# Mask building, load sizes and task order in an mLSTM and two-MoE kernel

## The chip, the core and the metric

The kernel runs on one core of a Trainium2 chip. The metric is the device time of one execution in microseconds, lower is better. The core has TensorE (matmuls, called PE in the profile, with its weight loads as PEld), VectorE (DVE), ScalarE (ACT), GpSimd (POOL) and SyncE (SP), which issues most of the DMAs. Each engine works through its own list of instructions in order.

## The reference

Three stages in a row. The first is a recurrence over 768 time steps, for 2 batches and 8 heads of dimension 40; the other two are gated feed-forward layers over 1536 tokens of width 320 with a hidden width of 1536.

```python
for t in range(S):
    m_new = np.maximum(f_gate[:, :, t] + m, i_gate[:, :, t])
    f_stab = np.exp(f_gate[:, :, t] + m - m_new); i_stab = np.exp(i_gate[:, :, t] - m_new)
    C = f_stab * C + i_stab * outer(v_t, k_t);    n = f_stab * n + i_stab * k_t
    y[:, :, t] = sigmoid(o_gate[:, :, t]) * (C @ q_t) / np.maximum(np.abs(n @ q_t), 1.0)
x = (sigmoid(x @ w_gate) * (x @ w_val)) @ w_out      # first layer
x = ((x @ w_a) * (x @ w_b)) @ w_out                  # second layer
```

The feed-forward weights are 8-byte floating-point numbers, handed to the kernel as 64-bit integers.

## The kernel before

The recurrence is worked in 12 steps of 64 time steps (T = 64), over all 16 pairs of batch and head at once. For step s the kernel loads keys and queries (`load_kq`, tile kq) and values and keys by token (`load_kv`, tile Y), and makes a matrix of decay exponents on TensorE (`ph_E`, line 404): a product of lhsE and rhsE, in which the gate values V of the step stand in blocks, one per head, so that a mask is part of the data. ScalarE takes the exponentials (`ph_exp`, line 412, tile Dt), TensorE the key-query products (`ph_S`), VectorE multiplies both (`ph_P`, line 460). With keys weighted by decay (`ph_kw`, line 415) TensorE updates the state (`ph_st`, copied on ScalarE by `ph_state`, line 491) and makes the outputs (`ph_o`, line 479). These are normalised and gated (`ph_norm`, `ph_norm2`, line 507), transposed (line 517) and stored as a high and a low part in xb.

The decay blocks are filled in two ways. For steps 0 and 1 `ph_prep` multiplies V by a mask on VectorE (lines 378 and 384). For the later steps `ph_place` copies V into the blocks by ten small DMAs for each pair of steps, eight for rhsE (line 397) and two for lhsE (line 400), on SP's queue. The tables lhsE and rhsE are first copied from constants (cs) by ScalarE (lines 726 and 732); before, the second pair is zeroed by GpSimd.

Key-query products have two forms: for steps below NQ the queries are added to the same result by two identity matmuls (line 435), and the product with Dt covers both; from NQ on the queries are multiplied by Dt separately (`ph_qg`, line 425).

Each of the 24 weight tiles (128 rows of hidden width, 12 for each layer) is loaded by three DMAs (`load_w`, lines 248 to 250, tile wst), turned from 8-byte numbers into 4-byte ones (`narrow1` on ScalarE, lines 258 and 259; `narrow2a` to `narrow2c` on VectorE or GpSimd, lines 265 to 282), and split into a high part (`split1`, ScalarE) and low parts (`split2`, `split3`, lines 298 to 303). A unit of the feed-forward layers is one weight tile against two or four blocks of 128 tokens: two chains of matmuls (line 554: pa and pb), gate and product on ScalarE and VectorE, and a third chain (lines 561 to 563: acc). The first 24 units (HEAD) have two token blocks and run among the recurrence's steps.

The order on every engine is not written by hand. All work is a list of tasks, each with engines it may run on, a duration in nanoseconds, predecessors, buffers and a due time computed from a few constants. `order_tasks` runs this list through a model at build time: it takes, of the tasks that are ready, the one with the earliest start plus a small weight on its due time, and chooses among the allowed engines. Ready DMAs form a queue of their own ("D") whose model has an issue time and a wire time. The order so found is the program; at run time each engine waits only for true dependences. Where the model leaves TensorE idle ahead of the first feed-forward unit, `fill` issues dummy matmuls (line 208).

Of the kernel before, what the change touches and what calls it, by code (L numbers as in the profile page):

```python
# [50 lines left out]
SDUE0, SDUE = 17.7, 5.582  # L51
UDUE0, UDUE = 45.1, 3.871
CDUE = (15.5, 14.5, -5.422, 36.2)
CLEAD = -3.653
GDUE = (-1.384, -0.546, 39.8)
PLEAD = 10.2
SWITCH = 100
NQ = 6
MMDUE = 11.5
FGAP = 80  # L60
NFILL = 1
VBIAS = 563.4
SOFT, SOFTMAX = 0.017, 2291.8

HOLD = {4: "O7", 5: "O8", 6: "O9", 7: "O10", 8: "O11", 9: "O11"}
EDUE = 32.6
# [3 lines left out]
OGDUE = (-59.6, 21.1)  # L70
IDUE = 28.1
# [16 lines left out]

def tile_shape(name):

    return {"S": "T" if name[1] == "T" else "S", "O": "T", "Q": "S"}.get(name[0])


def order_tasks(tasks, bufs):
# [3 lines left out]
    port = wire = 0.0  # L98
    shape = None
# [8 lines left out]
    while ready:  # L108
        best = None
        for name in ready:  # L110
            on, _, after, due, uses, lock = tasks[name]
            new, held = {}, []
# [8 lines left out]
            for e, dur in on.items():  # L121
                t = max([free[e]] + [end[a] + hop(engine[a], e) for a in (*after, *held)])
# [40 lines left out]
def kernel(  # L163
# [75 lines left out]
    def load_w(c):  # L239
        l, f = divmod(c, NF)  # L240
        w, wo = ((w1, wo1), (w2, wo2))[l]
        k = 2 if wide else 1
        t = stpool.tile([P, NW * k], I32 if wide else F32, tag="wst", name=f"wst{c}")
        wo = wo[f * P : (f + 1) * P, :]
        w = w[f]
        if wide:
            w, wo = w.bitcast(I32), wo.bitcast(I32)
# [3 lines left out]
        wst[c] = t  # L251
# [122 lines left out]
    def ph_prep(s, eng):  # L374

        c0 = s * T
        re, ld = rhsE[0][:, s], lhsE[0][:, s]
# [30 lines left out]
    def ph_exp(s, par):  # L408

        if par == 0:  # L410
            Dt[s] = a2.tile([P, 2, NPAIR, B, T], F32, tag="Dt", name=f"Dt{s}")
        nc.scalar.activation(Dt[s][:, par], Eps[s, par].rearrange("p (a b t) -> p a b t", a=NPAIR, b=B), AF.Exp)

    def ph_kw(s, par, eng):
# [3 lines left out]
            Dt[s][:, par, :, :, T - 1 : T].to_broadcast([P, NPAIR, B, D]),  # L418
# [269 lines left out]
    BUFS = {"acc": 2, "mm1": 2, "e": 2, "y": 2, "dt": 2, "kq": 3, "xt": 2, "xb": 3, "g": 2, "gh": 2, "gl": 2,  # L688
# [21 lines left out]
    def t_start():  # L710
        load_gates(0)
        nc.scalar.dma_start(cs[:, C_RE:], cst[:, C_RE:])
# [6 lines left out]
    def dma(name, size, fn, after=(), due=0.0, uses=(), parts=1):  # L719

        task(name, "D", 480.0 * parts, fn, after, due, uses, lock=size / 0.29)

    dma("start", 300.0, t_start, (), -100, parts=2)
    dma("ident", 66.0, t_ident, ("start",), -88)
    def t_lhs(i):
        nc.scalar.activation(lhsE[i], cs[:, C_LD : C_LD + 2 * P].unsqueeze(1).to_broadcast([P, 2, 2 * P]), AF.Copy)
        if i:
            nc.gpsimd.memset(lhsE[i][32:64, :, T : T + P].bitcast(F32), 0.0)

    def t_rhs(i):  # L730
        r = slice(32 * i, P)
        nc.scalar.activation(rhsE[i], cs[:, C_RE : C_RE + 512].unsqueeze(1).to_broadcast([P, 2, 512]), AF.Copy)
        if i:
            nc.gpsimd.memset(rhsE[i][0:32].bitcast(F32), 0.0)
# [11 lines left out]
    for i, (c0, n) in enumerate(GCH):  # L746
# [8 lines left out]
        task(f"ge{i}", "A", 420 + 2.1 * n, c2, [f"gd{i}"], due + 0.3)  # L755
        task(f"gc{i}", "V", 220 + 1.05 * n, c3, [f"ge{i}"], due + 0.4, lock=True)
    for i in range(1, NSTEP // 2):
# [3 lines left out]
        dma(f"pl{i}", 130.0, lambda i=i: ph_place(i), src + ["rhs1", "lhs1"] + old, sdue(s) - PLEAD, parts=10)  # L761

    for s in range(NSTEP):
# [4 lines left out]
        dma("kq" + n, 328.0, lambda s=s: load_kq(s), ["start"], d - 12, [("kq", [z + n for z in ("S", *zs)])], parts=2)  # L768
# [22 lines left out]
        task("M" + n, "V", 500, lambda s=s: ph_norm2(s), ["N" + n], d + 5.2, lock=True)  # L791
# [184 lines left out]
```

## Time and profile before

| | us |
|---|---|
| median of 3 runs | 491.75 |
| lowest, highest | 491.3, 492.38 |
| the profiled execution | 492.37 |
| its span | 490.6 |
| TensorE busy in the span | 470.3 |
| VectorE, ScalarE, GpSimd busy | 286.2, 248.3, 126.0 |

The span is the time from the first to the last instruction in the profile, and a part of the execution's own time. Busy times are summed over the whole span; dummy matmuls count as TensorE's busy time. The profile also has the clock that TensorE was granted (1.00 is 2.4 GHz, 0.50 is 1.2 GHz) and the DMA engines' share of work in each stretch.

### The profile page before, as it was taken

What the parts mean: (1) busy time and instruction counts of PE and PEld (TensorE: products, weight loads), DVE (VectorE), ACT (ScalarE), POOL (GpSimd) and SP (SyncE); (2) the same over time, 40 slices, a digit from 0 to 9 for tenths busy, and PEclk for the clock granted to TensorE, in tenths of its full rate; (3) what the DMA queues carried; (4) which work ended last, traced back from release to release, by engine and by line L of the source; (5) the groups of instructions that cost most, each with busy time, mean ns of one, the idle gap of its engine ahead of it and who ended that gap; (6) DMA issues with size and microseconds to landing.
All of it is one profiled execution on the core that took longest, in us unless ns stands there. A gap on an engine that the chain in (4) does not pass through costs nothing.

```text
span 490.6 us, 9058 instructions
## 1 busy us (share of the span) xinstructions
PE 470.3 (96%) x3545; PEld 408.7 (83%) x3550; DVE 286.2 (58%) x474; ACT 248.3 (51%) x460; POOL 126.0 (26%) x141
## 2 busy tenths in 40 slices
PE   9969499999999999999999999999999999999995
PEld 3546498899999888888888888888888888888885
DVE  4785598957676768656555566754466323324242
ACT  5964595774788655555562543553454222222220
POOL 2314366554233103344240322231202000000000
PEclk9999799999999999999999999999999999999999
DMA  8944543920203332222311022220220000001022
GB/s 202 261 130 110 148 133 103 221 81 2 82 1 95 122 107 81 82 80 82 131 53 59 2 87 76 80 82 0 82 80 2 0 2 0 1 0 44 11 55 53
DMA packets 18506, 37.06 MB, mean 76 GB/s; under 512 B 3040, under 2 KB 9696, under 8 KB 18464
## 3 DMA queue, kind: packets, MB, share of 16 engines
q1 hardware_dynamic: 18048, 35.74, 25.0%
q10 hardware_dynamic: 416, 0.74, 0.7%
q8 instruction: 28, 0.46, 0.4%
q14 instruction: 14, 0.11, 0.1%
HBM read 34.35 MB, written 1.97 MB: 74 GB/s over the span
## 4 chain that ended last, share of the span: by engine, by line
PE 82%; DMA 9%; SPq 2%; DVE 2%; POOL 2%; issue 1%; ACT 1%; POOLq 0%; ACTq 0%; DVEq 0%
PE pa L554 29%; PE pb L554 22%; PE acc L561 9%; PE acc L563 8%; PE acc L562 8%; DMA x2tok<-in_ogate_dram 4%; DMA wst<-in_wo_dram 3%; SPq L397 1%; DMA Y<-in_kv_dram 1%; PE o L479 1%; PE sp L450 1%; PE t L517 1%; PE first L208 1%; DMA cs<-in_cst_dram 1%; POOL Kw L415 1%
## 5 line engine op out<-in xcount | busy, mean ns | idle before, releaser
L554 PE MATMUL pa<-xb,W 128*128 128x512 f32 (+1 forms) x864 | 172.3, 345 | 0.0
L554 PEld LDWEIGHTS pa<-xb,W 128*128 128x128 f32 x864 | 137.3, 190 | 15.9
L554 PE MATMUL pb<-xb,W 128*128 128x512 f32 x480 | 119.6, 392 | 0.0
L590 ACT ACTIVATE gh<-g 128x512 fp32r<-128x512 f32 (+1 forms) x84 | 47.9, 570 | 129.8 <-PE acc L562 107.8
L554 PEld LDWEIGHTS pb<-xb,W 128*128 128x128 f32 x480 | 89.9, 188 | 19.3
L584 DVE TENSOR_TENSOR g<-g,pb 128x512 f32<-128x512 f32 x60 | 41.3, 688 | 88.0 <-PE pb L554 86.2
L561 PE MATMUL acc<-W,gh 128*128 128x320 f32 x288 | 89.8, 312 | 0.0
L563 PE MATMUL acc<-W,gl 128*128 128x320 f32 x288 | 89.0, 309 | 0.0
L562 PE MATMUL acc<-W,gh 128*128 128x320 f32 x288 | 88.9, 309 | 0.0
L595 DVE TENSOR_TENSOR gl<-g,gh 128x512 fp32r<-128x512 f32 x60 | 44.4, 740 | 55.2 <-ACT gh L590 55.2
L579 ACT ACTIVATE g<-pa 128x512 f32<-128x512 f32 x60 | 35.8, 597 | 55.3 <-PE pa L554 55.1
L561 PEld LDWEIGHTS acc<-W,gh 128*128 128x128 f32 x288 | 54.0, 187 | 2.7
L562 PEld LDWEIGHTS acc<-W,gh 128*128 128x128 f32 x288 | 54.0, 188 | 2.4
L563 PEld LDWEIGHTS acc<-W,gl 128*128 128x128 f32 x288 | 54.0, 188 | 0.1
L282 POOL TENSOR_TENSOR wst<-cva,wst 128x960 int32<-128x960 int32 x11 | 25.2, 2290 | 66.6 <-DVE cva L276 32.7
L302 POOL TENSOR_TENSOR W<-wst,W 64x128 fp32r<-64x128 f32 x24 | 17.1, 711 | 91.7 <-ACT W L293 76.8
L258 ACT ACTIVATE cva<-wst 128x960 f32<-128x960 f32 x24 | 25.8, 1075 | 12.0 <-DMA wst<-in_wo_dram 11.8
L276 DVE SCALAR_TENSOR_TENSOR cva<-wst,cva 128x960 int32<-128x960 int32 x24 | 29.8, 1240 | 0.4
L595 POOL TENSOR_TENSOR gl<-g,gh 128x256 fp32r<-128x256 f32 x24 | 20.3, 844 | 36.3 <-ACT gh L590 26.4
L208 PE MATMUL first<-zb 128*128 128x512 bf16 x94 | 24.6, 416 | 1.5 <-DVE zb L212 1.2
L292 ACT ACTIVATE W<-wst 128x832 fp32r<-128x832 f32 x24 | 22.9, 955 | 6.1 <-DVE wst L282 5.1
L259 ACT ACTIVATE wst<-wst 128x960 int32<-128x960 uint32 x24 | 25.9, 1080 | 0.0
(83 smaller groups left out, 481.5 us busy)
## 6 DMA issues: line engine op xcount, KB each, us to landing
wst<-in_w_dram SPq DMA_DIRECT2D x24, 512.0 KB
wst<-in_wo_dram SPq DMA_DIRECT2D x24, 320.0 KB
Y<-in_kv_dram SPq DMA_DIRECT2D x24, 162.0 KB
kq<-in_kqT_dram SPq DMA_DIRECT2D x24, 160.0 KB
wst<-in_w_dram SPq DMA_DIRECT2D x24, 128.0 KB
out_dram<-x2tok SPq DMA_DIRECT2D x12, 160.0 KB
x2tok<-in_ogate_dram SPq DMA_DIRECT2D x1, 1600.0 KB
rhsE<-V SPq DMA_DIRECT2D x40, 2.0 KB
```

What stands on the lines that cost most here:

```text
L208: nc.tensor.matmul(t, zb[:, 0:P], zb, start=True, stop=True)
L258: nc.scalar.activation(cva[0], hi.bitcast(F32), AF.Abs)
L259: nc.scalar.activation(lo, lo.bitcast(U32), AF.Copy, scale=2.0**-29)
L276: nc.vector.scalar_tensor_tensor(ai, hi, -0x40000000, ai, op0=ALU.bitwise_and, op1=ALU.bitwise_or)
L554: nc.tensor.matmul(dst, w[:, w0 : w0 + P], x[:, h, cb], start=(i == 0), stop=(i == 7))
L561: nc.tensor.matmul(a, gh[:, c], wh, start=st, stop=False)
L562: nc.tensor.matmul(a, gh[:, c], wl, start=False, stop=False)
L563: nc.tensor.matmul(a, gl[:, c], wh, start=False, stop=sp)
L579: nc.scalar.activation(t, pa, AF.Copy if l else AF.Sigmoid)
L584: nc.vector.tensor_tensor(t, t, pb, op=ALU.mult)
L590: nc.scalar.activation(gh, g, AF.Copy)
L595: eng.tensor_tensor(gl, g, gh.bitcast(F32), op=ALU.subtract)
```

## The change

1. Steps 0 to 5 (NPREP = 6) all have their decay blocks filled by `ph_prep`, on VectorE or on GpSimd. DMAs fill them for steps 6 to 11 alone. The second pair of tables is no longer zeroed.
2. A weight tile comes by one DMA; the three weights are packed side by side in memory. Keys and queries of a step come by one DMA of 104 rows (24 of them zeros) in place of two of 40.
3. The first gates are loaded first, then the constants, both on SP's queue (the constants were on ScalarE's). Table copies depend on the constants alone and may go to GpSimd; so may the second normalisation (`ph_norm2`).
4. The tile Dt is split into one for each of the two head parities. NQ goes from 6 to 7, so that step 6 takes the form with identity matmuls.
5. The model counts 560 ns for each DMA issue, holds at most ten DMAs in flight, and has new constants. A list (PLAN) then sets a due time for each of some 460 tasks, up to unit 31, and fixes the engine of some.
6. The number of dummies ahead of the first two TensorE tasks is the gap divided by 430 ns; for the others it stays the gap less 80 ns, divided by 215 ns.

```diff
-NQ = 6
+ISSUE, DEPTH = 560, 10
+NQ = 7
+NPREP = 6
+PLAN = """
+start:-1.6: cst:7.9: ident:-880.3: rhs0:-24.1:A lhs0:-56.3:A rhs1:14: lhs1:4.9:A yi0:-113.7:A yi1:10.1:
+yi2:-108.6:A og0:-838.8: sg0:15.6: og1:-838.7: sg1:1.4: ga0:-7.1: gb0:-5.6: gd0:-5.7: ge0:-61.4: gc0:15.3:
...
+E12:19.4: X12:63.7: P12:-770: k12:-63.8:G S2:27.9: ST2:69.2: st2:64.2: O2:27: N2:56: M2:34.9:G D2:31.4:
+T2:39.6: xh2:44.4: xl2:-0: kq3:-368.1: kv3:-373.6: pr3:-1.5:G E03:16.6: X03:38: P03:41.1: k03:-1.2: E13:10.7:
+X13:27.9: P13:33.1: k13:5:G S3:28.4: ST3:44.3: st3:51.9: O3:34.2: N3:81: M3:41.4:G D3:9.8: T3:48.1: xh3:12.9:
+xl3:38.1: kq4:-375.8: kv4:-377.8: pr4:34.3:V E04:54.7: X04:29: P04:24.7: k04:32.6:G E14:35.4: X14:34.3:
...
+"""
 def order_tasks(tasks, bufs):
...
+            again = 0.0
+            if "D" in on:
+                again = flight[min(-DEPTH + int(on["D"] / ISSUE) - 1, -1)]
...
     def load_w(c):
         l, f = divmod(c, NF)
-        w, wo = ((w1, wo1), (w2, wo2))[l]
+        w = (w1, w2)[l][f]
...
-        nc.sync.dma_start(t[:, 0 : 4 * P * k], w[:, 0 : 4 * P * k])
-        nc.sync.dma_start(t[:, NH * k :], w[:, 4 * P * k :])
-        nc.sync.dma_start(t[:, 4 * P * k : NH * k], wo)
+        nc.sync.dma_start(t, w.bitcast(I32) if wide else w)
...
-        for r in (0, 64):
-            nc.sync.dma_start(kq[s][r : r + D].rearrange("p x a b t -> p (x a b t)"), kqT[r // 64, :, s])
+        nc.sync.dma_start(kq[s][0 : 64 + D].rearrange("p x a b t -> p (x a b t)"), kqT[:, s])
...
-        re, ld = rhsE[0][:, s], lhsE[0][:, s]
+        re, ld = rhsE[s // 2 % 2][:, s % 2], lhsE[s // 2 % 2][:, s % 2]
...
-        nc.scalar.dma_start(cs[:, C_RE:], cst[:, C_RE:])
...
-    dma("start", 300.0, t_start, (), -100, parts=2)
+    dma("start", 66.0, t_start, (), -100)
+    dma("cst", 415.0, lambda: nc.sync.dma_start(cs[:, C_RE:], cst[:, C_RE:]), (), -95)
...
-        task(f"rhs{i}", "A", 1120, lambda i=i: t_rhs(i), ("ge0",), IDUE + i * 5)
-        task(f"lhs{i}", "A", 620, lambda i=i: t_lhs(i), ("ge0",), IDUE + i * 5 + 0.5)
+        task(f"rhs{i}", {"A": 1060, "G": 1500}, 0, lambda e, i=i: t_rhs(i, e), ("cst",), IDUE + i * 15)
+        task(f"lhs{i}", {"A": 620, "G": 800}, 0, lambda e, i=i: t_lhs(i, e), ("cst",), IDUE + i * 15 + 0.5)
...
-    for i in range(1, NSTEP // 2):
+    for i in range(NPREP // 2, NSTEP // 2):
...
-        if s < 2:
-            task("pr" + n, {"V": 960}, 0, lambda e, s=s: ph_prep(s, e), ["gc0", "rhs0", "lhs0"], d - PLEAD, lock=True)
+        if s < NPREP:
...
+            task("pr" + n, {"V": 960, "G": 1900}, 0, lambda e, s=s: ph_prep(s, e), src, d - PLEAD, lock=True)
...
-        task("M" + n, "V", 500, lambda s=s: ph_norm2(s), ["N" + n], d + 5.2, lock=True)
+        task("M" + n, {"V": 500, "G": 900}, 0, lambda e, s=s: ph_norm2(s, e), ["N" + n], d + 5.2, lock=True)
...
+    for entry in PLAN.split():
+        name, due, e = entry.split(":")
+        on, fn, after, _, uses, lock = tasks[name]
+        tasks[name] = ({e: on[e]} if e else on, fn, after, float(due), uses, lock)
...
-            n = int(gap / 430) if name == "E00" else int(max(gap - FGAP, 0) / 215)
+            n = int(gap / 430) if first is not None and nfill < 2 else int(max(gap - FGAP, 0) / 215)
```

## Rows read from the trace of the kernel before

**Rows 1.** Stretches: length, busy per engine (PE PEld DVE ACT POOL), PEclk, DMA, GB/s.

```profile
0.00:14.02 14.02, 12.82 (x47) 5.15 (x47) 6.20 (x19) 8.42 (x14) 3.62 (x7) 1.00 0.82 204
14.02:45.85 31.83, 26.36 (x402) 16.93 (x406) 24.27 (x45) 24.05 (x36) 11.12 (x13) 1.00 0.60 158
45.85:60.00 14.15, 7.52 (x129) 7.01 (x128) 7.22 (x14) 6.86 (x14) 4.50 (x5) 0.81 0.62 167
60.00:105.00 45.00, 43.33 (x715) 40.30 (x716) 38.34 (x71) 33.49 (x81) 25.53 (x30) 0.98 0.57 150
105.00:482.00 377.00, 377.00 (x2239) 336.23 (x2239) 207.68 (x324) 175.15 (x318) 81.19 (x88) 1.00 0.16 51
482.00:490.60 8.60, 3.30 (x23) 3.04 (x21) 2.51 (x5) 0.30 (x1) 0.00 (x0) 0.86 0.31 76
```

**Rows 2.** The same stretches, dummy matmuls of line 208 alone: PE, PEld, PEclk, DMA.

```profile
0.00:14.02 14.02, 12.82 (x46) 5.15 (x46) 1.00 0.82 204
14.02:45.85 31.83, 11.79 (x49) 4.53 (x52) 1.00 0.60 158
60.00:105.00 45.00, 0.75 (x2) 0.29 (x3) 0.98 0.57 150
```

**Rows 3.** Two shorter stretches, all instructions.

```profile
58.00:62.50 4.50, 4.50 (x42) 4.27 (x43) 4.49 (x9) 3.21 (x8) 2.45 (x4) 0.61 0.42 117
60.00:80.00 20.00, 19.93 (x399) 18.71 (x399) 18.57 (x35) 15.81 (x35) 13.26 (x15) 0.96 0.43 121
```

**Rows 4.** Timeline of TensorE: start, us, line, operation, [idle before, releaser].

```profile
15.42 0.81 PE L404 MATMUL e<-rhsE,lhsE 128*128 128x512 f32 x2
...
45.85 2.04 PE L554 MATMUL pa<-xb,W 128*128 128x256 f32 x16
...
57.78 0.90 PE L517 MATMUL tp<-cs,xt 128*128 128x128 f32 x3 [6.63 <-ACT Dt L412]
```

**Rows 5.** Timeline of ScalarE, and its waits for weights (in total, times, longest).

```profile
12.65 0.74 ACT L372 ACTIVATE x2tok<-x2tok 128x640 f32<-128x640 f32 x1 [1.21 <-DMA x2tok<-in_ogate_dram]
...
52.63 1.06 ACT L258 ACTIVATE cva<-wst 128x960 f32<-128x960 f32 x1 [7.72 <-DMA wst<-in_wo_dram]
...
ACT cva L258 <- DMA wst<-in_wo_dram: 11.8, 3, 7.7
```

**Rows 6.** Timeline of SP's queue: start, us of issuing, what.

```profile
27.16 6.34 SPq L397 DMA_DIRECT2D rhsE<-V  x8
...
36.22 5.57 SPq L397 DMA_DIRECT2D rhsE<-V  x8
...
45.42 0.53 SPq L248 DMA_DIRECT2D wst<-in_w_dram  x1
```

**Rows 7.** A group of VectorE's by line (count, busy, mean), then VectorE's and GpSimd's timelines.

```profile
L378 DVE TENSOR_TENSOR rhsE<-V,cs 32x512 fp32r<-32x512 f32 x2 | 1.4, 680 | 0.1
...
31.13 0.49 DVE L507 TENSOR_TENSOR xt<-xt,nrm 128x320 f32<-128x320 f32 x1
...
33.92 1.03 DVE L298 TENSOR_TENSOR W<-wst,W 128x832 fp32r<-128x832 f32 x1
...
42.74 1.48 DVE L507 TENSOR_TENSOR xt<-xt,nrm 128x320 f32<-128x320 f32 x1
...
41.62 2.26 POOL L282 TENSOR_TENSOR wst<-cva,wst 128x960 int32<-128x960 int32 x1
```

**Rows 8.** DMA issues with their sizes.

```profile
kq<-in_kqT_dram SPq DMA_DIRECT2D x24, 160.0 KB
...
x2tok<-in_ogate_dram SPq DMA_DIRECT2D x1, 1600.0 KB
```

**Rows 9.** Timeline of TensorE: key-query products of one step, in either form.

```profile
44.15 0.65 PE L435 MATMUL sp<-kq,cs 40*64 40x512 f32 x2
...
44.68 0.90 PE L450 MATMUL sp<-kq 40*64 40x64 f32 x16
...
88.68 1.15 PE L450 MATMUL sp<-kq 40*64 40x64 f32 x32
```

More of the change, by code (lines that the diff above doesn't have):

```diff
@@ L48, in hop @@
     return {"P": 200, "V": 125, "A": 145, "G": 75, "D": 0}[a] + (25 if b == "G" else 0)
[L51 to L56, printed above, removed]
+SDUE0, SDUE = 9.561, 6.941
+UDUE0, UDUE = 38.7, 5.349
+CDUE = (-5.757, 28.5, -6.571, 29.3)
+CLEAD = -27.6
+GDUE = (25.6, -50.4, 19.2)
+PLEAD = 2.433
 SWITCH = 100
-NQ = 6
-MMDUE = 11.5
+ISSUE, DEPTH = 560, 10
+NQ = 7
+NPREP = 6
+MMDUE = 12.3
 FGAP = 80
 NFILL = 1
-VBIAS = 563.4
-SOFT, SOFTMAX = 0.017, 2291.8
+VBIAS = -86.7
+SOFT, SOFTMAX = 0.007, 2850.3
 HOLD = {4: "O7", 5: "O8", 6: "O9", 7: "O10", 8: "O11", 9: "O11"}
-EDUE = 32.6
+EDUE = 12.5
 OGA = 2
 GCH = ((0, 128), (128, 320), (448, 320))
-OGDUE = (-59.6, 21.1)
-IDUE = 28.1
+OGDUE = (-74.9, 13.6)
+IDUE = 132.0
 NW = 5 * P + DM
@@ L98, in order_tasks @@
     port = wire = 0.0
+    flight = [0.0] * DEPTH
     shape = None
@@ L121, in order_tasks @@
             for e, dur in on.items():
-                t = max([free[e]] + [end[a] + hop(engine[a], e) for a in (*after, *held)])
+                t = max([free[e], again] + [end[a] + hop(engine[a], e) for a in (*after, *held)])
                 if e == "G" or e == "V" and lock:
@@ L150, in order_tasks @@
             end[name] = wire + 900
+            flight += [end[name]] * int(on[e] / ISSUE)
         order.append(name)
@@ L719, in dma, with t_copy, t_lhs, t_rhs @@
     def dma(name, size, fn, after=(), due=0.0, uses=(), parts=1):
-        task(name, "D", 480.0 * parts, fn, after, due, uses, lock=size / 0.29)
-    dma("start", 300.0, t_start, (), -100, parts=2)
+        task(name, "D", ISSUE * parts, fn, after, due, uses, lock=size / 0.29)
+    dma("start", 66.0, t_start, (), -100)
+    dma("cst", 415.0, lambda: nc.sync.dma_start(cs[:, C_RE:], cst[:, C_RE:]), (), -95)
     dma("ident", 66.0, t_ident, ("start",), -88)
[L725 to L734, printed above, removed]
+    def t_copy(e, out, x):
+        if e is None:
+            nc.scalar.activation(out, x, AF.Copy)
+        else:
+            e.tensor_copy(out, x)
+    def t_lhs(i, e):
+        t_copy(e, lhsE[i], cs[:, C_LD : C_LD + 2 * P].unsqueeze(1).to_broadcast([P, 2, 2 * P]))
+    def t_rhs(i, e):
+        t_copy(e, rhsE[i], cs[:, C_RE : C_RE + 512].unsqueeze(1).to_broadcast([P, 2, 512]))
     for i in range(2):
-        task(f"rhs{i}", "A", 1120, lambda i=i: t_rhs(i), ("ge0",), IDUE + i * 5)
-        task(f"lhs{i}", "A", 620, lambda i=i: t_lhs(i), ("ge0",), IDUE + i * 5 + 0.5)
+        task(f"rhs{i}", {"A": 1060, "G": 1500}, 0, lambda e, i=i: t_rhs(i, e), ("cst",), IDUE + i * 15)
+        task(f"lhs{i}", {"A": 620, "G": 800}, 0, lambda e, i=i: t_lhs(i, e), ("cst",), IDUE + i * 15 + 0.5)
     for i in range(3):
-        task(f"yi{i}", {"A": 940, "G": 1200}, 0, lambda e, i=i: y_init(i, e), ("start",), sdue(i) + 1.5)
+        task(f"yi{i}", {"A": 940, "G": 1200}, 0, lambda e, i=i: y_init(i, e), ("cst", "start"), sdue(i) + 1.5)
     for i, (s0, s1) in enumerate(((0, OGA), (OGA, NSTEP))):
@@ L754 @@
         task(f"gd{i}", "V", 360 + 2.8 * n, c, [f"gb{i}"], due + 0.2, lock=True)
-        task(f"ge{i}", "A", 420 + 2.1 * n, c2, [f"gd{i}"], due + 0.3)
+        task(f"ge{i}", "A", 420 + 2.1 * n, c2, [f"gd{i}", "cst"], due + 0.3)
         task(f"gc{i}", "V", 220 + 1.05 * n, c3, [f"ge{i}"], due + 0.4, lock=True)
-    for i in range(1, NSTEP // 2):
+    for i in range(NPREP // 2, NSTEP // 2):
         s = 2 * i
@@ L775 @@
             task(f"X{p}{n}", "A", 600, lambda s=s, p=p: ph_exp(s, p), [f"E{p}{n}"], d + 0.5,
-                 [("dt", [z + n for z in (*zs, "k0", "k1")])] if p == 0 else [])
+                 [(f"dt{p}", [f"{z}{p}{n}" for z in ("P", "k", *(("q",) if s >= NQ else ()))])])
             task(f"P{p}{n}", "V", 700, lambda s=s, p=p: ph_P(s, p), ["S" + n, f"X{p}{n}"] + back("O", 2), d + 2)
@@ L865 @@
             if e == "P" and first is not None:
+                nfill += 1
                 fill(first, n)
@@ L870 @@
     ps_stack.close()
-_INS = ["gates", "cst", "kqT", "kv", "ogate", "w1", "wo1", "w2", "wo2"]
+_INS = ["gates", "cst", "kqT", "kv", "ogate", "w1", "w2"]
 def _layout(inputs):
```

117 lines of the change are left out of this document (86 added, 31 removed).

## The prediction

> **What bounds the kernel now.** Read the stretches first, then what each engine waits for inside the bad ones. TensorE is without a gap from 105 to 482 us: 377.00 busy of 377.00 at a granted clock of 1.00 [rows 1]. Nothing in that stretch can be gained by moving DMAs, VectorE or GpSimd work; only TensorE's work itself would count there, and the change leaves it as it is. So the time is set by how much of the first 105 us TensorE spends on something other than the kernel's work, plus a tail of 8.60 - 3.30 = 5.30 us.
>
> In the first 105 us a busy TensorE is not yet a useful one, because the kernel issues dummy matmuls (line 208) while it waits. Subtract them [rows 2] from the busy time [rows 1]:
> - 0 to 14.02 us: nothing useful, 14.02 lost.
> - 14.02 to 45.85: 26.36 busy, 11.79 of it dummies, so 14.57 useful and 17.26 lost.
> - 45.85 to 60: 7.52 of 14.15, so 6.63 lost.
> - 60 to 105: 43.33 busy with 0.75 dummies, so 45.00 - 42.58 = 2.42 lost.
>
> That is 40.33 us; with the tail, 45.63 of the 490.6 us span. On top, TensorE runs from 58 to 62.5 us at a mean granted clock of 0.61 after the idle stretch [rows 3], which is 4.5 x 0.39 = 1.8 us. So at most 42.1 us lie ahead of the saturated part, and some of that is the unavoidable first load and recurrence.
>
> Why it is lost. The first decay exponents (line 404) run at 15.42 and the first expert matmul at 45.85 [rows 4]. ScalarE stands until 12.65 for the output gates [rows 5], and only behind them in its order comes the left mask table (line 726), without which these exponents can't run. The third weight is issued on SP's queue only at 45.42, behind two blocks of mask DMAs: 27.16 to 33.50 and 36.22 to 41.79 for the eight right-side pieces alone, with two left-side pieces after each [rows 6]. ScalarE, which works in order, meets that weight's first copy 7.72 us before it has landed, at 52.63 [rows 5]; exponentials and state copies of the recurrence are behind it in the order, and TensorE stands 6.63 us, until 57.78 [rows 4]. So one late DMA on a crowded queue costs 6.63 us and the 1.8 us of slow clock.
>
> **The change, part by part.** (1) Mask DMAs of steps 2 to 5 go: 20 issues. Eight took 6.34 us and 5.57 us in the two blocks [rows 6]. This frees about 14 us of SP's queue with the left-side pieces (estimate: ten pieces at 0.6 to 0.8 each, twice). Three weight loads become one and two key/query loads become one, so a step with a weight has three issues less, about 0.55 each as the weight's first [rows 6]. The third weight's slot is free when the first weight's split ends on VectorE, at 33.92 + 1.03, about 35 us [rows 7]; the queue was the later of the two, by about 10 us. With the queue free that 7.72 us wait of ScalarE goes, and its price, 6.63 + 1.8 = 8.4 us, with it, unless what is late next takes its place: VectorE, below.
>
> (2) In place of these DMAs come four mask products, each a 32x512 and a 32x128 multiply: 0.680 us on VectorE for the larger [rows 7] and, by its size, less than half of that for the smaller, so under 1 us each: 4 us if all are on VectorE, nothing to VectorE if all are on GpSimd. The plan pins step 4's to VectorE and step 3's to GpSimd and leaves two open. Steps 2 and 3's normalisation (0.49 us, [rows 7]) move to GpSimd. Step 6's two query products go, from VectorE or GpSimd. Net, VectorE gets between -2 and +3 us; I take +1, since one mask at least is VectorE's and work on GpSimd is not always free for VectorE.
>
> That last point is weighed by a row: the same VectorE multiply takes 0.49 us at 31.13 and 1.48 us at 42.74, when GpSimd runs a 2.26 us addition begun at 41.62 [rows 7]. The Trainium skill, "SBUF — State Buffer", section "SBUF: two separate sides", says that VectorE instructions with two SBUF inputs and GpSimd instructions lock each other out of a shared port for a whole instruction; the row agrees, VectorE's multiply ends with GpSimd's. By that rule each move to GpSimd can cost VectorE up to GpSimd's own duration; with three moves, none as large as the shown addition of 2.26 us, the sum would be up to 7 us worse than by busy time alone (an estimate).
>
> (3) Gates and constants come first and the output gates later; table copies of ScalarE wait for the constants alone, not for the first gate chain. That takes the 12.65 us wait from ahead of the first exponents: the exponents could run at 10 to 11 us. But the first weight (960 KB) is now ahead of step 0's keys in the queue, and at 204 GB/s [rows 1] the 2.4 MB up to these keys take about 12 us. So I take the first useful step 3 us sooner (between 0 and 5). The key/query load carries 416 KB in place of twice 160 [rows 8]: 96 KB at 204 GB/s are 0.5 us a step, hidden except in the first two steps; these lie in the 3 us. The Trainium skill, "DMA: Bandwidth & Descriptors", section "Why a DMA increments its semaphore by 16 and not by 1", has the number of DMA engines as the largest divisor, up to 16, of the row counts: 10 for 40 rows, 13 for 104. By that the merged load would put eight rows on each engine as the two loads did, and cost nothing; no row here shows the engines of one load.
>
> (4) Step 6 now uses the form with two identity matmuls. On TensorE this form takes from 44.15 to 45.58, 1.43 us, against 1.15 us for the other at 88.68 [rows 9]: +0.3 us, in full on the path.
>
> (5) The new order and engine of each task. No row prices this; it is bounded by VectorE, the busiest engine beside TensorE. In the first 105 us it works 6.20 + 24.27 + 7.22 + 38.34 = 76.03 us: 63% of the time up to 60 us, 85% from 60 to 105, and 18.57 of 20 (93%) in its densest 20 us [rows 1, 3]. Call "saturated" the state that is reached at 105 us now, and ask when VectorE can have done the same 76.03 + 1 us. Let the first 14.02 us with their 6.20 us of VectorE work shrink to 11.0 (part 3). The remaining 70.8 us at 85% take 83.3 us, so 94.3 us and 10.7 gained; at 93% 76.1 us, so 87.1 us and 17.9 gained. Low end: 80% gives 99.5, 5.5 gained. I take 14.4, the middle of 85% and 93%, since 85% was reached with the mask blocks of three later step pairs still in the queue, and the new kernel has the same three.
>
> Sum: 14.4 - 0.3 = 14.1 us. TensorE's own losses check it: 3.0 (start) + 6.6 (stand) + 1.8 (clock) = 11.4 without anything from the 17.26 us of the stretch between; the rest, 2.7, is a sixth of it. Both sums hold the 377 us stretch and the tail as they are. The profiled execution took 492.37 us, 1.8 more than its span; the median of the runs is 491.75. I set the gain against the median: 477.7 us.
>
> **The rivals.** *Late weights again.* ScalarE stays in order, and the order is a fixed list. The second output-gate load (1600 KB, [rows 8]) still stands ahead of the second weight in the queue, 8 us at 204 GB/s. If ScalarE meets weights before they land, exponents stand behind, as now: 8.4 us for the 7.72 us wait. In all ScalarE waits 11.8 us for weights now [rows 5]. Two such stalls cost 16.8 us against the 14.1: 494.5 us. It ends slower than now once new waits for weights, over what the sum assumes (none), pass about 13 us. For it: the list has hundreds of entries whose order holds only if the durations do. Against it: the queue has far fewer issues. *VectorE takes no more than now*: if it stays near 72% because chains, not the queue, leave it idle, the gain is the start alone or nothing: 491 us. *The order fits very well*: VectorE at 93% over everything and the start 5 us sooner, 20 to 25 us gained: 469 us.
>
> **How the numbers follow.** Forecast, 6 to 20 us gained: 0.60. Very good fit, over 20 us: 0.17. No difference: 0.06. Late weights: 0.17. Faster by over 0.2% (about 1 us, what a measurement of this kernel can tell from none): 0.60 + 0.17 = 0.77; same 0.06; slower 0.17. The range goes from 467, most of the good fit, to 490, which takes in the low end of the VectorE bound (486) and a part of weaker gains; it leaves out the slower case, no difference and the best of the good fit.
>
> **What would show it.** Right: the first expert matmul near 30 us, no TensorE stand of several us about 50, granted clock 1.00 from there, TensorE without a gap from about 90 us, VectorE at 85 to 93% between. The dummies should fall from 25 us. Wrong: ScalarE waiting over 13 us for weights; VectorE's share up to saturation as low as now; or TensorE gaps after 105 us, which would mean that a weight or a split comes too late in the steady part, of which no row of now warns.

## The result, and the profile after

The changed kernel takes 485.12 us (median; 482.5 to 486.4) against 492.06 us for the kernel before on the same chip: a ratio of 0.9853, 95% interval 0.9807 to 0.99. It is faster, by 6.9 us; forecast were 14.1. The profiled execution took 484.31 us with a span of 482.2, against 492.37 and 490.6 before.

The same kind of stretches as in [rows 1], cut at the changed kernel's own events: first useful matmul, first expert matmul, 60 and 105 us, and the tail (length; busy time of PE, PEld, DVE, ACT, POOL; granted clock; DMA share; GB/s):

```profile
0.00:15.05 15.05, 8.29 (x28) 3.18 (x29) 9.19 (x23) 8.55 (x14) 5.96 (x10) 0.91 0.79 206
15.05:41.80 26.75, 24.01 (x379) 15.90 (x380) 22.03 (x44) 18.49 (x29) 9.85 (x11) 0.86 1.00 243
41.80:60.00 18.20, 17.76 (x335) 16.05 (x334) 17.40 (x37) 15.95 (x34) 11.90 (x12) 1.00 0.55 152
60.00:105.00 45.00, 43.18 (x583) 41.30 (x582) 35.45 (x71) 30.09 (x75) 19.71 (x17) 0.92 0.46 125
105.00:475.00 370.00, 370.00 (x2180) 329.12 (x2179) 214.11 (x345) 171.97 (x306) 41.78 (x54) 1.00 0.16 53
475.00:482.20 7.20, 1.94 (x14) 1.67 (x12) 1.81 (x4) 0.00 (x0) 0.00 (x0) 0.84 0.37 91
```

The dummy matmuls alone (line 283 now) in the first four of these stretches:

```profile
0.00:15.05 15.05, 8.29 (x28) 3.15 (x28) 0.91 0.79 206
15.05:41.80 26.75, 8.89 (x28) 2.86 (x28) 0.86 1.00 243
41.80:60.00 18.20, 0.78 (x2) 0.19 (x2) 1.00 0.55 152
60.00:105.00 45.00, 0.38 (x1) 0.10 (x1) 0.92 0.46 125
```

Counted as in the prediction, the loss is now 15.05 up to the first useful matmul (14.02 before), 26.75 - 24.01 + 8.89 = 11.63 up to the first expert matmul (17.26), 18.20 - 17.76 + 0.78 = 1.22 up to 60 us (6.63), 45.00 - 43.18 + 0.38 = 2.20 up to 105 (2.42) and 5.26 in the tail (5.30). In all 35.36 us against 45.63: 10.3 us less. But the span fell by 8.4 only, so the useful work itself takes 1.9 us longer. That is clock above all: the granted clock is 0.92 from 60 to 105 us, where it was 0.98, and 0.86 from 15.05 to 41.80, where the kernel before had 1.00 up to its first expert matmul [rows 1].

So half of what the loss fell by is where it was expected, in the stand about 50 us. The head got shorter by much less than forecast: the first expert matmul came at 41.80 us, where it was at 45.85 and was expected near 30. Two numbers of the rows above point to the reason before any experiment: VectorE is 81% busy up to 60 us ((9.19 + 22.03 + 17.40) / 60), but the DMA engines are busy throughout from 15 to 41.8 us, at a share of 1.00, where they stood at 0.60 before [rows 1].

TensorE's timeline (start, length, [idle before, what ended it]):

```profile
15.05 1.12 PE L501 MATMUL sp<-kq,cs 40*64 40x512 f32 x2 [5.58 <-DMA kq<-in_kqT_dram]
...
25.10 1.10 PE L545 MATMUL o<-Y,Z 128*64 128x41 f32 x32
...
40.10 0.65 PE L501 MATMUL sp<-kq,cs 40*64 40x512 f32 x2 [1.54 <-DMA kq<-in_kqT_dram]
...
70.84 1.32 PE L535 MATMUL st<-Y,Kw 128*40 128x41 f32 x32 [1.74 <-DVE Kw L481]
```

SP's queue (start, time of issuing), and then three transfers on the chain that ends last (start, time until landed):

```profile
2.70 0.59 SPq L319 DMA_DIRECT2D wst<-in_w_dram  x1
...
5.08 1.62 SPq L428 DMA_DIRECT2D kq<-in_kqT_dram  x1
...
31.61 0.53 SPq L319 DMA_DIRECT2D wst<-in_w_dram  x1
```

```profile
5.08 9.85 DMA kq<-in_kqT_dram
...
28.72 11.34 DMA kq<-in_kqT_dram
...
56.18 11.47 DMA Y<-in_kv_dram
```

The third weight (31.61) is issued 13.8 us sooner than before [rows 6]. But step 0's keys stand behind the first weight and take 9.85 us to land, step 3's keys take 11.34 and step 7's values 11.47; each has TensorE or VectorE waiting at its end. The state matmul at 70.84 waits for VectorE's product of those values; VectorE makes it in two halves, begun at 67.75 and 69.56, and its order has some 1.5 us of other work between them.

### The profile page after: what moved, and what is told of

The parts are those of the page before. It is cut to its first block, busy times and chain, and to the rows that moved or that the text cites. A ratio compares the mean times of both kernels' runs of the same rounds, so it can differ in the third digit from the quotient of the medians.

```text
span 482.2 us, 8785 instructions
## 1 busy us (share of the span) xinstructions
PE 465.2 (96%) x3511; PEld 407.2 (84%) x3511; DVE 300.0 (62%) x519; ACT 245.1 (51%) x455; POOL 89.2 (18%) x103
## 4 chain that ended last, share of the span: by engine, by line
PE 90%; DMA 7%; DVE 1%; POOL 1%; SPq 1%; issue 0%; DVEq 0%; POOLq 0%
PE pa L620 31%; PE pb L620 23%; PE acc L627 9%; PE acc L629 9%; PE acc L628 9%; DMA kq<-in_kqT_dram 4%; DMA Y<-in_kv_dram 2%; PE sp L516 2%; PE o L545 2%; PE st L535 1%; PE e L471 1%; PE first L283 1%; PE t L583 1%; POOL Y L779 1%; PE tp L583 1%; DVE x2tok L735 0%
## 5 line engine op out<-in xcount | busy, mean ns | idle before, releaser
L661 DVE TENSOR_TENSOR gl<-g,gh 128x512 fp32r<-128x512 f32 (+1 forms) x77 | 50.3, 654 | 48.8 <-ACT gh L656 48.4
L370 POOL TENSOR_TENSOR W<-wst,W 64x128 fp32r<-64x128 f32 x19 | 16.0, 844 | 131.7 <-ACT W L361 129.3
L344 DVE SCALAR_TENSOR_TENSOR cva<-wst,cva 128x960 int32<-128x960 int32 x24 | 27.7, 1153 | 0.3
L366 DVE TENSOR_TENSOR W<-wst,W 128x832 fp32r<-128x832 f32 x23 | 23.7, 1029 | 1.7 <-ACT W L360 1.6
L735 DVE SCALAR_TENSOR_TENSOR x2tok<-acc,x2tok 128x320 f32<-128x320 f32 x52 | 23.0, 482 | 2.7 <-PE acc L629 2.7
L350 DVE CUSTOM_DVE_ANT_0 wst<-wst,cva 128x1920 uint16<-128x1920 uint16 x19 | 21.9, 1154 | 0.5
```

What stands on the lines that cost most here:

```text
L344: nc.vector.scalar_tensor_tensor(ai, hi, -0x40000000, ai, op0=ALU.bitwise_and, op1=ALU.bitwise_or)
L366: e.tensor_tensor(w[:, NH : 2 * NH], g[:, 0:NH], w[:, 0:NH].bitcast(F32), op=ALU.subtract)
L661: eng.tensor_tensor(gl, g, gh.bitcast(F32), op=ALU.subtract)
```

## The experiments

The median of the kernel before lay between 491.42 and 492.06 us in all these series; ratios are to it, with their 95% intervals.

**Part 1 of the change alone (e9_masks_alone).** On the kernel before: the two blocks of mask DMAs become mask products, in their places.

```diff
-        re, ld = rhsE[0][:, s], lhsE[0][:, s]
+        re, ld = rhsE[s // 2 % 2][:, s % 2], lhsE[s // 2 % 2][:, s % 2]
...
+            if name in ("pl1", "pl2"):
+                s = 2 * int(name[2])
+                ph_prep(s, nc.vector)
+                ph_prep(s + 1, nc.gpsimd)
+            else:
+                tasks[name][1](eng.get(e))
```

> The kernel before with part 1 of the change alone: the masks of steps 2 to 5 are multiplied where the two blocks of mask DMAs stood in its order (steps 2 and 4 on VectorE, 3 and 5 on GpSimd); order, engines, loads and start stay those of before. Step 1 of the prediction priced the freed queue at 8.4 us (6.63 us of stand and 1.8 us of slow clock), and putting these DMAs back into the changed kernel cost 10.7 us. Theory A (the freed queue is the gain, whatever the order): 481 to 484 us, with the third weight issued near 35 us and no stand of TensorE over 3 us about 50 us. Rival B (the gain needs the new order, which was searched with these masks on VectorE and GpSimd; the old one has VectorE meet them at bad places, or ScalarE waits for the weight all the same): 488 to 492 us.

Measured: 483.05 us, ratio 0.9823 [0.9801, 0.9844]. Theory A holds: 8.5 us gained, where step 1 (part 1 of the prediction) said 8.4. SP's queue, and the stretch that takes the place of the stand of 6.63 us:

```profile
37.06 0.36 SPq L248 DMA_DIRECT2D wst<-in_w_dram  x1
```

```profile
43.79:60.00 16.21, 15.23 (x296) 14.06 (x295) 15.02 (x30) 13.69 (x29) 10.62 (x12) 1.00 0.46 132
```

The third weight goes out at 37.06 instead of 45.42 [rows 6], TensorE loses 1.4 us in that stretch, a dummy of 0.38 counted, and its clock stays at 1.00. This part alone takes 2.1 us less than the whole change, but the intervals overlap: at least as good is what the runs show.

The 8.4 and the 8.5 aren't the same sum, though. Counted as above, e9's span is 9.3 us shorter (481.3 against 490.6): 5.3 in the stand, 2.1 because the useful work takes less time, as it would without the slow clock behind the stand, 1.5 ahead of the first expert matmul, which comes at 43.79, and 0.4 elsewhere. Step 1 has nothing for the part ahead of that matmul. The stretch up to it in e9, all of it and its dummies, and TensorE's waits for mask pieces in the kernel before (total, times, longest), which e9 doesn't have:

```profile
13.21:43.79 30.58, 27.86 (x405) 17.43 (x405) 28.29 (x49) 25.00 (x39) 15.14 (x17) 0.94 0.80 223
13.21:43.79 30.58, 13.87 (x53) 4.71 (x52) 0.94 0.80 223
```

```profile
PE e L404 <- DMA lhsE<-V: 3.3, 2, 2.4
```

**The mask DMAs put back into the changed kernel (e3_mask_dmas).** The order stays that of the change; steps 2 and 4's mask products become the DMA blocks of their pairs, steps 3 and 5's go.

```diff
-            tasks[name][1](eng.get(e))
+            if name in ("pr2", "pr4"):
+                ph_place(int(name[2]) // 2)
+            elif name not in ("pr3", "pr5"):
+                tasks[name][1](eng.get(e))
```

> The changed kernel with the masks of steps 2 to 5 made by DMAs again: in the same order of everything else, two blocks of ten small DMAs stand in SP's queue where the first mask product of each pair stood, and VectorE and GpSimd make four masks fewer. Theory A (the queue freed of 20 DMAs is what the change gains): the third weight is issued some 10 us later than 31.61 again, ScalarE or TensorE stands behind it, and most of the gain goes, 490 to 496 us. Rival C (the gain is the order; masks cost the same in either place): 485 us within 2 us.

Measured: 495.87 us, ratio 1.0079 [1.005, 1.0108], so 10.7 us slower than the changed kernel. SP's queue and TensorE's longest wait (total, times, longest):

```profile
24.50 13.14 SPq L464 DMA_DIRECT2D rhsE<-V  x8
45.99 0.53 SPq L319 DMA_DIRECT2D wst<-in_w_dram  x1
46.58 5.56 SPq L464 DMA_DIRECT2D rhsE<-V  x8
```

```profile
PE e L471 <- DMA lhsE<-V: 12.1, 1, 12.1
```

The third weight is back at 45.99, and TensorE waits 12.1 us for a mask piece. The path differs from that of the kernel before: ScalarE waits only 0.2 us for weights up to 110 us, so here it is the masks themselves that are late, and what step 1 says of the third weight rests on e9 alone. From both sides the mask DMAs are where the gain of this change is; the rest of it, in its own order with these DMAs put in, is slower than the kernel before.

**The merged loads (e4_split_loads, e7_split_w, e8_split_kq, e12_single_loads).** In the changed kernel the weight's load is cut in three again (e7), the key/query load in two (e8), or both (e4); the order stays.

```diff
-        nc.sync.dma_start(t, w.bitcast(I32) if wide else w)
+        w = w.bitcast(I32) if wide else w
+        for a, b in ((0, 4 * P), (NH, NW), (4 * P, NH)):
+            nc.sync.dma_start(t[:, a * k : b * k], w[:, a * k : b * k])
...
-        nc.sync.dma_start(kq[s][0 : 64 + D].rearrange("p x a b t -> p (x a b t)"), kqT[:, s])
+        for r in (0, 64):
+            nc.sync.dma_start(kq[s][r : r + D].rearrange("p x a b t -> p (x a b t)"), kqT[r : r + D, s])
```

> The changed kernel with three DMAs for a weight tile and two of 40 rows for a step's keys and queries again, same order. Both theories: more issues on SP's queue, about 1.1 us for a weight and 0.4 us for a step, but 96 KB less for each step's keys on the wire. Theory A: 0 to 2 us slower than the changed kernel, 485 to 487. Rival B (the wire sets the head): the smaller key loads count, 0.4 us for each of five steps, 483 to 485.

> The changed kernel with three DMAs for a weight tile again, keys and queries in one DMA as changed, same order. With both split the time was 481.33 us. If the three smaller weight loads bring that gain (smaller loads let the keys behind them in sooner): 481 to 482 us. If the 96 KB of zeros in each key load cost it: 485 us within 1 us.

> The changed kernel with two DMAs of 40 rows for keys and queries again, one DMA for a weight as changed, same order. The other half of the pair: 481 to 482 us if the zeros on the wire cost the 3.8 us that splitting both gained; 485 us within 1 us if the weight loads do.

Measured: both 481.33 us, 0.9794 [0.9762, 0.9826], 3.8 us faster than the changed kernel by the medians and 2.9 by the ratios, with intervals that overlap a little; weights alone 483.42, 0.9823 [0.9793, 0.9852]; keys alone 482.11, 0.9802 [0.9777, 0.9828]. Neither alone is told apart from the changed kernel, nor one from the other, and the two don't add up (1.7 + 3.0 against 3.8). In these traces the head is no shorter than the changed kernel's 41.80: the first expert matmul comes at 42.02 (both), 43.28 (weights) and 43.43 (keys). What differs stands behind it. From 70 to 80 us the granted clock is 1.00 in all three, where the changed kernel has 0.66, and 10 x 0.34 is 3.4 us. That stretch in e4 and e7, and the stand of e7 in it:

```profile
70.00:80.00 10.00, 9.16 (x144) 8.79 (x145) 9.42 (x25) 6.31 (x19) 4.32 (x5) 1.00 0.54 164
70.00:80.00 10.00, 7.78 (x133) 7.21 (x134) 9.43 (x23) 5.95 (x16) 6.07 (x5) 1.00 0.40 125
```

```profile
72.24 0.81 PE L537 MATMUL st<-Y,Kw 128*40 128x41 f32 x32 [1.75 <-DVE Kw L483]
```

Between executions of the same mean granted clock (0.985 to 0.987) there is less: the one of the changed kernel took 482.50 us, the five of e4 480.68 to 481.79. So in the new order it is not shown that the merged loads cost 3.8 us. To see whether it is the loads or the order in which they stand, e12 takes the kernel with the masks alone (e9) and merges its loads as the change does:

```diff
-        nc.sync.dma_start(t[:, 0 : 4 * P * k], w[:, 0 : 4 * P * k])
-        nc.sync.dma_start(t[:, NH * k :], w[:, 4 * P * k :])
-        nc.sync.dma_start(t[:, 4 * P * k : NH * k], wo)
+        nc.sync.dma_start(t, w.bitcast(I32) if wide else w)
...
-        for r in (0, 64):
-            nc.sync.dma_start(kq[s][r : r + D].rearrange("p x a b t -> p (x a b t)"), kqT[r // 64, :, s])
+        nc.sync.dma_start(kq[s][0 : 64 + D].rearrange("p x a b t -> p (x a b t)"), kqT[:, s])
```

> The kernel with the masks alone (483.05 us), and its loads merged as in the change: one load per weight tile, one key/query load of 104 rows with zeros between; the order is that of the kernel before. In the changed kernel, splitting these loads again gained 3.8 us. Theory A (the merged loads themselves cost, by the zeros that they carry and by how they sit on the DMA engines): 485 to 488 us in this order too. Rival B (they cost only in the new order, where the weight stands ahead of the first keys and the DMA engines are full from 6 to 42 us): 482 to 484 us.

Measured: 487.13 us, 0.9907 [0.9879, 0.9934]: 4.1 us slower than e9, and the two intervals don't touch. Theory A's time holds: in the old order the merged loads cost 4.1 us. Its reasons, the zeros and the place on the DMA engines, are not shown; the rows point to another. First e9: SP's queue at step 1's keys and at the second output-gate load, then ScalarE at the first output gates and the first exponential:

```profile
6.98 5.93 SPq L361 DMA_DIRECT2D kq<-in_kqT_dram  x2
...
14.19 0.59 SPq L369 DMA_DIRECT2D x2tok<-in_ogate_dram  x1
```

```profile
12.62 0.74 ACT L372 ACTIVATE x2tok<-x2tok 128x640 f32<-128x640 f32 x1 [1.42 <-DMA x2tok<-in_ogate_dram]
...
16.65 1.09 ACT L412 ACTIVATE Dt<-e 128x512 f32<-128x512 f32 x2
```

Then the same in e12:

```profile
5.26 0.55 SPq L351 DMA_DIRECT2D kq<-in_kqT_dram  x1
...
9.25 0.41 SPq L359 DMA_DIRECT2D x2tok<-in_ogate_dram  x1
```

```profile
14.95 0.74 ACT L362 ACTIVATE x2tok<-x2tok 128x640 f32<-128x640 f32 x1 [3.73 <-DMA x2tok<-in_ogate_dram]
...
18.98 0.60 ACT L402 ACTIVATE Dt<-e 128x512 f32<-128x512 f32 x1
```

In e9 the pieces of step 1's keys hold SP's queue for 5.93 us, and the 1600 KB of output gates that nobody needs yet go out at 14.19. With two loads in the place of five the queue gets through, those 1600 KB go out at 9.25, and the 320 KB that ScalarE does need, issued on ScalarE's queue at 4.1 us in both kernels, land 2.3 us later. ScalarE works in order, so its first exponential is 2.3 us later too, and the first expert matmul comes at 47.36 instead of 43.79. That the bulk in flight slows the small load is argued from these times; a kernel with the merged loads and that one load held back wasn't run.

**Dummies in place of the stand (e1_warm).** 28 dummies more ahead of the first useful matmul, so that the clock stays up.

```diff
+                n += 28 * (nfill == 0)
                 nfill += 1
```

> The changed kernel, same order, with 28 more dummy matmuls ahead of the first key-query products (56 in place of 28), so that TensorE does not stand for 5.58 us before the keys land at 15.05 and its clock is not at 0.50 from 12 to 22.6 us. Theory A (the lost half of the forecast lies at the start: a late start at a slow clock): first products 1.45 us in place of 2.38, the 13 dummies 2.8 us in place of 3.9, step 0's outputs about 2 us sooner, 1.5 to 2.5 us off the end, so about 483 us. Rival B (the wire sets the head: later keys land when they land, step 3's at 40.06): clock 1.00 there, but the end within 0.5 us of 485.

Measured: 487.45 us, 0.9898 [0.9863, 0.9933]: no gain, and not told apart from the changed kernel. Two stretches of it and two rows of its TensorE:

```profile
30.00:46.00 16.00, 12.66 (x180) 9.74 (x174) 12.71 (x28) 9.91 (x19) 4.46 (x5) 0.89 0.88 221
...
70.00:80.00 10.00, 8.02 (x94) 7.44 (x91) 8.57 (x17) 4.77 (x12) 5.66 (x5) 0.66 0.31 92
```

```profile
39.96 0.65 PE L501 MATMUL sp<-kq,cs 40*64 40x512 f32 x2 [1.98 <-DMA kq<-in_kqT_dram]
...
72.22 1.32 PE L535 MATMUL st<-Y,Kw 128*40 128x41 f32 x32 [1.98 <-DVE Kw L481]
```

Step 0 ran at full clock and ended 2 us sooner, and step 3 still waited for its keys until 39.96 us (40.10 without the dummies). So the slow clock at the start is not what makes step 3 late: the loads set when it can run. What step 0 gained went into longer stands, and the one at 72.22 has a slow clock behind it again.

**The keys ahead of the first weight (e2_keys_first).** In the planned list, `after(a, n)` moves the tasks n to right behind a: the weight's load, then its narrowing.

```diff
+        after("kq0", "w0")
+        after("X00", "na0")
+        after("P10", "nb0", "ns0", "nc0", "nd0")
```

> The changed kernel with the first weight's load moved behind step 0's keys in SP's queue, and that weight's narrowing moved behind step 0's exponentials on ScalarE and VectorE; the rest in the same order. The weight's 960 KB at 230 GB/s are 4.2 us, so step 0's keys land near 11 us in place of 15.05, and TensorE stands 1.5 us in place of 5.58, with its clock kept. Theory A: step 0's outputs at 18 to 20 us in place of 25.10 and 3 to 5 us off the end, about 481 us. Rival B: the first products move, the first expert matmul (41.80) and the end do not, 485 us within 1 us.

Measured: 481.67 us, 0.9778 [0.9747, 0.9808]: 3.5 us faster than the changed kernel, and the intervals only just touch. The place of the first weight and of its narrowing, which moved together, costs about that.

**Keys issued by need (e5_kq9_later, e6_kq_by_need).** Step 9's keys behind step 8's values (e5); also step 3's keys ahead of step 4's (e6).

```diff
+        after("kv8", "kq9")
+        after("w1", "kq3")    # e6 only
+        after("kv3", "kq4")   # e6 only
```

> The changed kernel with one load moved: step 9's keys and queries go behind step 8's values in SP's queue, in place of ahead of step 7's; all else in the same order. In the changed kernel step 7's values are issued at 56.18 and land 11.5 us later, TensorE stands 1.74 us for them at 69 us, and its clock is 0.50 to 0.57 from 70 to 76 us. Theory D (loads out of order of need on a full wire, and the clock that a short stand costs): 416 KB less ahead, 1.8 us sooner, the stand gone, the clock kept: 1.7 + 3 us, 480 to 482 us. Rival E (VectorE and the chain of state updates set this place anyway): 485 us within 1 us, with the stand still there.

> As the kernel before it here, and besides step 3's keys are loaded ahead of step 4's; the changed kernel has them the other way round, and TensorE stands 1.54 us for step 3's keys until 40.06, right ahead of the first expert matmul (41.80). Theory D: first expert matmul 1.5 us sooner, 1.5 us off the end on top: 479 to 480.5 us. Rival E: the first expert matmul moves, the end does not: the same as the kernel before it here, within 1 us.

Measured: 484.04 us, 0.9829 [0.9792, 0.9867], and 482.46, 0.983 [0.9787, 0.9873]. Neither is told apart from the changed kernel by time. In e5's trace the stand at step 7 is 1.14 us, shorter but not gone. The trace of e6 does show what was aimed at: no wait at step 3, and no stand in this stretch, where the changed kernel has 18.18 busy of 20:

```profile
60.00:80.00 20.00, 20.00 (x303) 19.00 (x302) 18.24 (x38) 16.21 (x42) 9.41 (x10) 1.00 0.68 177
```

Ahead of it the same trace lost what it gained there: a new stand of 2.06 us ends at 30.41, the clock is 0.76 from 15 to 42 us, and the first expert matmul comes at 42.78, later than the changed kernel's.

**All of these together (e10_all_four).** The moves of e2 and e6 and the split loads of e4 in one kernel.

> The changed kernel with all that gained alone: step 0's keys loaded ahead of the first weight (481.67 us alone), weight loads in three and key/query loads in two pieces (481.33 us), keys of steps 3 and 9 issued by need (482.46 us), against 485.12 us for the changed kernel. Theory A (each takes away another wait of the head): the gains of 3.5, 3.8 and 2.7 us add up to 10.0, in part: 475 to 478.5 us, no wait of TensorE for keys over 1.5 us after the first step. Rival B (the DMA engines are the bound of the first 42 us, so that whichever load comes first only moves the wait to another): 480 to 483 us, as each alone.

Measured: 478.07 us, 0.9727 [0.9705, 0.975]: 7.0 us faster than the changed kernel and 13.5 faster than the one before, the fastest of all. Theory A holds: 7.0 of the 10.0. Three rows of its TensorE:

```profile
9.34 1.74 PE L504 MATMUL sp<-kq,cs 40*64 40x512 f32 x3 [0.52 <-DMA kq<-in_kqT_dram]
...
24.55 1.18 PE L474 MATMUL e<-rhsE,lhsE 128*128 128x512 f32 x2 [3.98 <-DVE lhsE L454]
...
38.28 1.10 PE L623 MATMUL pa<-xb,W 128*128 128x256 f32 x8
```

The first key products run at 9.34 us instead of 15.05, the first expert matmul at 38.28 instead of 41.80, and the longest wait left is 3.98 us for step 2's mask, a VectorE product. None of these edits adds or removes any arithmetic. About half of the 7 us is head: the first expert matmul is 3.5 us sooner, by the order and the cut of the loads and by where the first weight's narrowing stands. The other half is clock: 1.00 from 60 to 80 us, where the changed kernel has 0.83, which is 20 x 0.17 = 3.4 us.

**The next block of mask DMAs too (e11_no_pl3).** As e10, with steps 6 and 7's masks multiplied as well.

```diff
+            if name in ("pl3",):
+                s = 2 * int(name[2])
+                ph_prep(s, nc.vector)
+                ph_prep(s + 1, nc.gpsimd)
+            else:
+                tasks[name][1](eng.get(e))
```

> As the kernel with all four edits, and the masks of steps 6 and 7 too are multiplied (step 6 on VectorE, step 7 on GpSimd) where their block of mask DMAs stood (41.98 us in the changed kernel, eight issues in 6.98 us, so some 9 us of SP's queue). Theory A (this queue time still holds up loads that are due, the values of step 7 first): 1 to 3 us faster than the kernel with all four edits, the keys of step 7 issued before 48 us. Rival B (VectorE, 79 to 93% busy there, pays for one mask product what the queue gives back): within 1 us of it, or up to 1 us slower.

Measured: 479.31 us, 0.9753 [0.9729, 0.9776], 1.2 us more than e10, with intervals that overlap. Theory A fell; B is not refuted. GpSimd's last split of the second weight and SP's queue at the fourth, in e11 and then in e10:

```profile
50.07 1.13 POOL L373 TENSOR_TENSOR W<-wst,W 64x128 fp32r<-64x128 f32 x1
51.23 1.47 SPq L321 DMA_DIRECT2D wst<-in_w_dram  x3
```

```profile
48.19 0.76 POOL L373 TENSOR_TENSOR W<-wst,W 64x128 fp32r<-64x128 f32 x1
48.98 1.30 SPq L321 DMA_DIRECT2D wst<-in_w_dram  x3
```

With the block of mask DMAs gone, the fourth weight goes out no sooner: the queue was not what it waited for. There are two buffers for weights, and in both kernels the load goes out 0.03 us after GpSimd is done with the second weight (51.20 and 48.95); in e11 the queue issues nothing from 40.62 until then. A freed queue is worth something only where the load behind it has a free buffer and somebody late for it.

## Why the prediction was half right, step by step

**Step 1, the freed queue: right in mechanism, in size partly by luck.** Forecast 8.4 us; alone it gave 8.5 (e9), and taken out of the change it cost 10.7 (e3, by another path). In e9 the third weight, the stand about 50 us and its slow clock behaved as the prediction said, but they make 7.4 of the 9.3 us of span; most of the rest came ahead of the first expert matmul, where the sum had not counted the waits for mask pieces. That the measured time lies among the 6 to 20 us of the forecast is due to this step; all the others together gave nothing that is told apart from zero.

**Step 3, the merged loads: mis-sized, nothing forecast beyond what lies in the start, 4.1 us measured.** "96 KB at 204 GB/s are 0.5 us a step, hidden except in the first two steps" counted bytes, and part 1 took the fewer issues for a pure gain. They cost 4.1 us in the old order (e12). In the new one it is 2.9 to 3.8 us that is not clear of the noise (e4), and in the traces it is clock and not head. The prediction weighed the rule of the Trainium skill, "DMA: Bandwidth & Descriptors", section "Why a DMA increments its semaphore by 16 and not by 1", by which the number of engines leaves eight rows to each either way and the merged load is free. No run here shows the engines of one load, so the rule itself stands untested. That merging costs nothing does not hold in e12, whose rows point to when the other loads are let go, of which engine counts say nothing; e12 merges weights and keys together, so the keys' share of it is not known.

**Step 3, the start: failed.** Forecast 3 us sooner (0 to 5); the first key products came 1.0 us later (15.05 against 14.02) and step 0's output matmul 6.0 us later (25.10), where the kernel before had

```profile
19.13 1.13 PE L479 MATMUL o<-Y,Z 128*64 128x41 f32 x32
```

The prediction saw that the first weight now stood ahead of step 0's keys and priced it by 2.4 MB at 204 GB/s, 12 us, and still took a gain. The keys landed at 15. e2 puts the price of that place, with the narrowing's, at 3.5 us.

**Steps 3 to 5, the new order: 1.4 to 2.7 us instead of 5.7.** The forecast of 14.1 leaves 14.1 - 8.4 = 5.7 for order, engines, start and step 6's form. By the ratios, order and start give 0.9907 - 0.9853 = 0.54% with merged loads (2.7 us) and 0.9823 - 0.9794 = 0.29% with split ones (1.4 us), both smaller than their intervals. Along the runs, by ratios, the masks give 1.77%, the merged loads take 0.84 and the order gives 0.54: 1.47% in all, as measured, though only because the last is what was left over. The record of the executions shows one thing that the new order pays with: the mean granted clock is 0.994 to 0.999 in the four executions of e9 and 0.974 to 0.986 in the four of the changed kernel. Over their spans that gives up 0.5 to 2.9 us and 6.7 to 12.6 us, some of it while TensorE stood or ran dummies.

**Step 5, VectorE as the bound: the step that failed.** To "ask when VectorE can have done the same 76.03 + 1 us" needed VectorE to be what is short. It was 81% busy up to 60 us in the changed kernel (63% before), close to the 85 that the sum began from, and the first expert matmul still came at 41.80 rather than near 30. The DMA engines, at a share of 1.00 from 15 to 42 us, were short: in e1 step 0 ended 2 us sooner, and step 3 waited for its keys until the same time. [Rows 1] had them at 0.82 and 0.60 while VectorE stood at 44% and 76%, so shares alone would have named them for the first stretch only. Bytes say more: the kernel before moves 204 x 14.02 + 158 x 31.83 KB, 7.9 MB, up to its first expert matmul, and at 243 GB/s, the most in the stretches of the changed kernel, these take 32 us (an estimate, as if all were needed by then), so "near 30 us" left no room. With the loads in another order and cut (e10), VectorE reaches 84% up to 60 us and the time is 478.07, while the DMA share is still 0.95 from 15 to 42 us. That points to which load comes first more than to how full the DMA engines are; the two were not told apart.

**Step 2, the mask products: small, as said.** The lock of VectorE and GpSimd appears at one mask. A left-side piece on VectorE, alone and beside GpSimd's product of another mask, and that product:

```profile
16.15 0.28 DVE L451 TENSOR_TENSOR lhsE<-V,cs 32x128 fp32r<-32x128 f32 x1
...
24.44 1.27 DVE L451 TENSOR_TENSOR lhsE<-V,cs 32x128 fp32r<-32x128 f32 x1
...
23.79 1.77 POOL L445 TENSOR_TENSOR rhsE<-V,cs 32x512 fp32r<-32x512 f32 x1 [1.20 <-DVE V L418]
```

0.28 us becomes 1.27, and VectorE ends at 25.71, just after GpSimd at 25.56. The rule of the Trainium skill, "SBUF — State Buffer", section "SBUF: two separate sides", that the two lock each other out of a shared port for a whole instruction, agrees with this row: about 1 us at this mask. The other moves in the estimate of 7 us were not priced.

**The rivals.** New waits of ScalarE for weights, the slower case, did not come: ScalarE waits for no weight's load up to 110 us. The waits that did come were for keys and values, which no rival named.

**Granted clock.** Forecast 1.00 from the end of the stand on. The stand about 50 us is gone, but a new one of 1.74 us ends at 70.84, and the clock goes with it (2-us stretches):

```profile
70.00:72.00 2.00, 1.16 (x32) 1.16 (x32) 1.99 (x3) 1.31 (x4) 2.00 (x2) 0.57 0.04 8
72.00:74.00 2.00, 2.00 (x39) 1.84 (x35) 1.84 (x3) 0.89 (x2) 1.56 (x3) 0.50 0.01 1
74.00:76.00 2.00, 2.00 (x10) 1.96 (x9) 1.76 (x6) 0.00 (x0) 0.72 (x1) 0.50 0.32 86
76.00:78.00 2.00, 2.00 (x14) 2.00 (x13) 1.33 (x3) 1.32 (x4) 0.00 (x0) 0.73 0.75 207
```

Over these 8 us the granted clock gives up 2 x (0.43 + 0.50 + 0.50 + 0.27) = 3.4 us, twice the stand itself; that is most of the 45 x 0.08 = 3.6 us lost from 60 to 105. What came as said: TensorE has no gap worth the name from 80 us on, and the dummies fell from 25.4 to 18.3 us.

## What to carry to other kernels

Before an engine is taken as the bound of a stretch, compare its busy share with the DMA share of the same stretch, and the bytes that must land in it with the rate the DMA engines reach. When a change frees an issuing queue, ask what it will let go sooner and which small, urgent load must then share the DMA engines with it. Fewer and larger DMAs are no gain by themselves: a queue that was held up by many pieces may have kept bulk loads back at just the right time. When a large re-plan is mixed with one clear removal, run the removal alone; here it was worth at least as much as the whole. And before a gain of 3 us is put down to an edit of the head, compare the granted clock behind the head in both traces.

## What the hardware showed that was not expected

Issuing the same eight 2 KB pieces on SP's queue took from 5.56 to 13.14 us within one kernel (e3), and the DMA share of the two stretches, 0.65 and 0.69, does not tell them apart. And the price of a short stand in clock is not fixed: after 1.74 us without work at 70.84 the clock was at the lower of its two levels (0.50, 1.2 GHz) for about 6 us, while the stand of 1.54 us that ended at 40.10 was followed by a stretch at 1.00 throughout (41.80 to 60, above). Nor is it the length alone: in e7 a stand of 1.75 us at the same state matmul (72.24, above) left the clock at 1.00. What tells them apart was not tried. The mean granted clock of the four executions of the changed kernel goes from 0.974 to 0.986, and the fastest (482.50 us) has the highest, but the slowest (486.40, at 0.982) not the lowest, so the clock explains only in part why they lie further apart than one would like for effects of 2 us.
